# Squares behind the first turned tiles, held token loads, and other numbers for the planner, in a two-layer attention and feed-forward kernel

## The chip, the cores and the metric

The kernel runs on one core of one Trainium2 chip. A core has five engines with a queue of instructions each: PE (TensorE, matrix products), DVE (VectorE), ACT (ScalarE), POOL (GpSimd) and SP (SyncE, which here only starts DMAs). Each works its own queue strictly in order; semaphores make one engine wait for another or for a DMA. The metric is the time of one execution on the device, in microseconds (us), as the median of several runs.

## The reference, cut to what matters

Two equal layers over x, 2048 tokens by 576. Each layer adds a sliding, dilated attention and then a feed-forward network with SiLU:

```python
x = x + _A_ref(_layernorm(x), A_wqkv, A_wo)
x = x + _B_ref(_layernorm(x), B_w1, B_w2)
x = x + _A_ref(_layernorm(x), A_wqkv, A_wo)
x = x + _B_ref(_layernorm(x), B_w1, B_w2)

# _A_ref: 32 heads of 18; each token looks at 8 tokens, itself and every second one before it
logits = einsum("bhsd,bhswd->bhsw", q, kg) * scale     # then softmax over w
o = einsum("bhsw,bhswd->bhsd", attn, vg)               # then o @ wo
# _B_ref: silu(x @ w1) @ w2, with 4608 hidden features
```

All data are float32.

## The kernel before, in words

**Tiles and stages.** The 2048 tokens are four chunks of 512 (blocks of even and odd tokens), each of four tiles of 128. A stage `s` counts chunks over both layers, 0 to 7: `front(s)` does layer norm, attention and projection, `ffn(s)` the feed-forward network. Products need float32's accuracy from float16 operands, so every operand is split in a high half (ACT, `hi`) and a low half, the residue (DVE, `lo` or `halves_lo` at L344); each product is then three passes, 14 matrix instructions for a 128-token tile ("a product" below).

**Weights of attention.** `wqkv` is cut into four units of eight heads. `raw_wq(u)` loads a unit in five pieces (the last in two halves), squares each on ACT (L474), sums the squares on PE (L480), takes a power-of-two scale `su` on DVE (L484 to 486), and splits the pieces (hi L491 on ACT, lo L494 on DVE). Buffers: units 0 and 1 lie raw in `h` tiles and split in `wq` tiles; unit 2 is split into the `wo` tile, unit 3 into `h` tiles.

**Layer norm.** `layer_norm` takes statistics on DVE (L384, L385), an inverse root by Newton steps on DVE, then per tile y (ACT L431 or DVE L423), yh's halves (ACT L434 and DVE L344, or all DVE), and turns the tile: `transposed` either does nine 128x128 turns on PE (L357) with a copy by ACT (L359), or one turning DMA on SP (L361). `PE_LN` says which, for chunks 0 to 3 of layer 1. y and yh have two buffers each.

**Stage 0 computes ahead.** Beside chunk 0's own attention, the queries, keys and values of chunks 1 to 3 are computed with each unit's weights (`qkv_ahead`, products L566, evictions L579) and stored to DRAM. For chunk 0 each unit's keys (`kv`) get a halo by four DMAs that ACT starts (L645), and DVE does the logits (multiply L664, sum L668, twice), softmax and the weighted values (L697, L704, L705). Then come projection (`project`, L736), layer norm, and FFN 0, which loads and splits w1 and w2 while it runs (`raw_load`, `raw_split`) and stores the halves; later FFNs load them (L748, L753). A product with w1 is a "z" (L861, 14 instructions), one with w2 a group of 18 (L882, "mm2").

**What sets the order.** Nothing is written in its final order. `op(engine, duration, fn, reads, writes, prio, nbytes, after)` records an operation with an estimated duration; `Plan.order()` then plays a list schedule with these estimates: an engine takes the ready operation of lowest `prio` for which buffers are free. DMAs are played too: they start `DMA_IN` after their issue, share `DMA_RATE` between queues, and land `DMA_OUT` after their last byte. The order in which operations start in this play is the order in which they are emitted, and each engine then keeps its part of it. `after` only bars an operation from starting earlier in the play; on the chip only true dependencies are waited for. `gate` lists layer norm's low halves, `marks` small copies on POOL that do read data and so do hold POOL's queue.

Of the kernel before, what the change touches and what calls it, by code (L numbers as in the profile page):

```python
# [16 lines left out]
P = 128  # L17
# [8 lines left out]
NJ = 4  # L26
# [24 lines left out]
class Plan:  # L51
# [4 lines left out]
    DMA_IN, DMA_OUT = 1.2, 0.9  # L56
    DMA_RATE = 0.33e6
# [174 lines left out]
def sliding_attention_silu_ffn(ctx: ExitStack, tc: tile.TileContext, x, wqkv, wo, w1, w2, out):  # L232
# [8 lines left out]
    def fl(t):  # L241
        return t.rearrange("p a b -> p (a b)")
# [5 lines left out]
    def T(b):  # L248
        return S.tags[b.tag][b.slot]
# [98 lines left out]
    def transposed(src, dst, key, j, prio, on_pe=False):  # L348


        if on_pe:
            m = Buf("acc")

            def turn():
                t = fl(T(m).bitcast(F16))
                for k in range(9):
                    nc.tensor.transpose(t[:, k * P:(k + 1) * P], T(src)[:, k, :], ident)  # L357
            op("PE", 0.8, turn, [(src, 0), (src, 1)], [m], prio)
            return op("ACT", 1.05, lambda: nc.scalar.activation(  # L359
                dst(), fl(T(m).bitcast(F16))[:, 0:9 * P].rearrange("p (a b) -> p a b", a=9), AF.Copy), [m], [(key, j)], prio - 9)  # L360
        return op("SP", 1.7, lambda: nc.sync.dma_start_transpose(dst(), fl(T(src))), [(src, 0), (src, 1)], [(key, j)], prio,  # L361
                  nbytes=P * 9 * P * 4)


    PE_LN = (1, 1, 1, 0)
# [95 lines left out]
    def raw_wq(u):  # L461
# [4 lines left out]
        for k in range(5):  # L466
            def load(k=k):
                d = raw(k).rearrange("p (t c) -> p t c", t=3)
                for p0, n, row in ((0, P, k * P),) if k < 4 else ((0, 64, 512), (64, 64, 512)):
                    (nc.sync if u else nc.scalar).dma_start(d[p0:p0 + n], wqkv[row:row + n, :].rearrange(  # L470
                        "p (t c) -> p t c", t=3)[:, :, u * UC:(u + 1) * UC])

            def square(k=k):
                nc.scalar.activation(junk[:, :QR], raw(k), AF.Square, accum_out=accq[:, u, k:k + 1])  # L474
            op("SP" if u else "ACT", 0.8 if k < 4 else 1.3, load, [], [rs[k]], WQ[u] if u else -20, nbytes=P * 3 * UC * 4, after=gate[3:4] if u > 1 else ())
            op("ACT", 0.8, square, [rs[k]], [("accq", u, k)], WQ[u])
# [120 lines left out]
    def attention(s, xT, wq, more=None):  # L597
# [4 lines left out]
        for u in range(NU):  # L602
# [11 lines left out]
            else:  # L614
# [13 lines left out]
                for j in range(NJ):  # L628
                    m = Buf("misc")

                    def evac(j=j, m=m, u=u, kv=kv, qt=qt):
                        d = du[:, u:u + 1]
                        nc.scalar.activation(T(kv)[:, j + W - 1].rearrange("p a b -> p (a b)"), T(m)[:, UC:3 * UC],  # L633
                                             AF.Copy, scale=d)
                        nc.scalar.activation(T(qt)[:, j, :], T(m)[:, 0:UC], AF.Copy, scale=d)
                    op("PE", 2.7 if s else 2.9, lambda j=j, m=m, w=w: qkv_matmul(xT, w, j, m),
                       [(xT, j)] + w.keys, [m], pr_)
                    op("ACT", 0.9, evac, [m, ("su", u)], [(kv, j), (qt, j)], pr_ - (0 if s else 9))
# [73 lines left out]
    def project(s, o, xs):  # L712

        pr_ = s - 1.0
        for j in range(NJ):
# [22 lines left out]
            op("PE", 3.5, mm, [(oT, j)] + [(WO, k) for k in range(10)], [acc], pr_)  # L738
# [94 lines left out]
    def ffn(s, xT, xs):  # L833
# [4 lines left out]
        for g in range(NFT // n):  # L838
# [8 lines left out]
            for f in range(g * n, (g + 1) * n):  # L847
# [14 lines left out]
                op("PE", 3.05, mm, [(xT, j) for j in range(NJ)] + ka, [z], pp)  # L862
# [8 lines left out]
            for j in range(NJ):  # L871
# [4 lines left out]
                for hs_ in ((0,), (1,)) if last else ((0, 1),):  # L876
                    for t in range(0, n, step):
# [7 lines left out]
                        op("PE", 0.37 * step * len(hs_), mm2, [(hb[q], a) for q in range(t, t + step) for a in range(2)]  # L885
# [48 lines left out]
    def front(s):  # L934
        X[s] = load_x(s, s - 1.0 if s else -20)
        if s == 0:
            no_keys()
            xT = layer_norm(X[0], -20, "xa", 3, PE_LN[0])
            x1 = layer_norm(load_x(1, -8.5, gate[0:1]), -8.5, "xb", False, PE_LN[1])
# [6 lines left out]
            o = attention(0, xT, raw_wq, more)  # L946
# [48 lines left out]
```

## Time and profile before

| | |
|---|---|
| median of 3 runs | 2225.29 us (2223.28 to 2235.29) |
| the profiled execution | 2231.58 us, of which 2229.8 us span |
| PE busy | 2180.4 us, 98% |
| DVE busy | 1393.3 us, 62% |
| ACT busy | 747.4 us, 34% |
| POOL busy | 206.3 us, 9% |

The durations come from the profiled execution. Busy shares are means over stages: the page's slices show DVE at 8 or 9 tenths over the first fifth of the span and lower later. In a timeline a row gives start, length, engine, line, operation, output and input tiles, and in brackets how long the engine idled before it and what ended that.

### The profile page before, as it was taken

Reading aid. Unit: us, or ns where it says so; the run is one execution under the profiler, and the core shown is the slowest. Engines: PE = TensorE matmul, PEld = TensorE weight load, DVE = VectorE, ACT = ScalarE, POOL = GpSimd, SP = SyncE. Lnnn points to the kernel's source line nnn. Section 1 sums busy time; section 2 is a strip of 40 time slices with the busy share of each in tenths; the row PEclk is TensorE's granted clock in tenths of the full one; section 3 lists DMA queues with packets and bytes.
Section 4 is the critical chain, followed back from the end, with each engine's and each line's share of the span. In section 5 each row is a group of like instructions: output and inputs, shape, how many; then the busy total and the mean of one; then the engine's idle time right before and its main releaser. Section 6 shows DMA issues by size and latency. Waiting matters only on the chain.

```text
span 2229.8 us, 33919 instructions
## 1 busy us (share of the span) xinstructions
PE 2180.4 (98%) x13858; PEld 1350.7 (61%) x13858; DVE 1393.3 (62%) x2047; ACT 747.4 (34%) x1211; POOL 206.3 (9%) x341
## 2 busy tenths in 40 slices
PE   5999999999999999999999999999999999999999
PEld 3556565656666666655666656666666566666665
DVE  7999989889988311359834597336971389511111
ACT  6455777543132122224212232222322223222222
POOL 2133555200001000000000000000000000000000
PEclk9999999999999999999999999999999999999999
DMA  5577667784645433455445454454453643433331
GB/s 152 165 206 274 235 224 240 200 231 155 184 152 154 116 103 105 150 128 178 116 112 160 103 176 121 125 159 131 135 132 120 167 140 117 91 115 123 112 113 40
DMA packets 220564, 332.18 MB, mean 149 GB/s; under 512 B 107240, under 2 KB 127572, under 8 KB 216440
## 3 DMA queue, kind: packets, MB, share of 16 engines
q1 hardware_dynamic: 191408, 230.47, 36.4%
q0 software_dynamic: 20704, 78.02, 10.3%
q10 hardware_dynamic: 8296, 21.52, 3.5%
q8 instruction: 108, 1.77, 0.3%
q14 instruction: 48, 0.39, 0.1%
HBM read 240.08 MB, written 47.03 MB: 129 GB/s over the span
## 4 chain that ended last, share of the span: by engine, by line
PE 85%; DVE 6%; DMA 4%; issue 2%; ACT 1%; POOL 1%; ACTq 0%; SPq 0%; DVEq 0%; POOLq 0%
PE z L861 36%; PE acc L882 34%; PE misc L566 7%; PE acc L736 4%; PE z L566 3%; DMA w<-in_B_w_dram 1%; DVE pr L664 1%; DMA kv<-kv 1%; DVE pr L697 1%; DVE lg L668 1%; DMA oT<-yh 1%; DMA h<-in_A_wqkv_dram 1%; DVE x L743 0%; DVE w L807 0%; DVE pr L704 0%
## 5 line engine op out<-in xcount | busy, mean ns | idle before, releaser
L861 PE MATMUL z<-xb,w 128*128 128x512 f16 x4032 | 882.8, 380 | 7.9 <-issue 3.9
L882 PE MATMUL acc<-w,h 128*128 128x288 f16 x6912 | 856.1, 286 | 2.2 <-DVE h L868 1.3
L882 PEld LDWEIGHTS <-h 128*128 128x128 f16 x6912 | 676.4, 98 | 179.9 <-DVE h L868 1.6
L861 PEld LDWEIGHTS <-w 128*128 128x128 f16 x4032 | 394.8, 98 | 475.7 <-issue 6.7
L863 ACT ACTIVATE hs<-z,d 128x512 f32<-128x512 f32 x288 | 197.6, 686 | 979.9 <-PE z L861 962.2
L868 DVE SCALAR_TENSOR_TENSOR h<-hs,sh,h 128x512 f16<-128x512 f32 x288 | 213.8, 748 | 311.7 <-ACT h L865 311.6
L743 DVE SCALAR_TENSOR_TENSOR x<-acc,d,x 128x576 f32<-128x576 f32 x135 | 109.9, 814 | 325.1 <-PE acc L882 325.0
L664 DVE TENSOR_TENSOR pr<-qt,kv 128x2304 f32<-128x2304 f32 x64 | 163.3, 2551 | 89.3 <-DMA kv<-kv 66.4
L865 ACT ACTIVATE h<-hs,sh 128x512 f16<-128x512 f32 x288 | 207.5, 721 | 9.4 <-DVE d L830 0.3
L566 PEld LDWEIGHTS <-xa 128*128 128x128 f16 x1344 | 131.7, 98 | 121.2 <-issue 7.1
L566 PE MATMUL misc<-wq,xa 128*128 128x432 f16 x1008 | 190.0, 349 | 3.8 <-ACT xa L359 2.5
L697 DVE TENSOR_TENSOR pr<-kv,pe 128x1152 f32<-128x1152 f32 x128 | 169.0, 1352 | 1.2
L668 DVE TENSOR_REDUCE lg<-pr 128x128 f32<-128x2304 f32 x64 | 163.1, 2548 | 1.2
L704 DVE TENSOR_TENSOR pr<-pr 128x1152 f32<-128x1152 f32 (+1 forms) x128 | 135.1, 1056 | 3.5
L736 PE MATMUL acc<-wo,oT 128*128 128x288 f16 x896 | 114.8, 288 | 4.6 <-DMA oT<-yh 4.6
L736 PEld LDWEIGHTS <-oT 128*128 128x128 f16 x896 | 88.3, 99 | 30.1 <-DMA oT<-yh 4.9
L633 ACT ACTIVATE kv<-misc,du 128x288 f32<-128x288 f32 x80 | 40.0, 500 | 138.5 <-PE misc L566 79.6
L906 POOL DMA_DIRECT2D out_dram<-x x12 | 6.5, 546 | 698.3 <-DVE x L743 698.3
L687 ACT ACTIVATE pe<-lg 128x256 f32<-128x256 f32 x32 | 13.3, 416 | 169.2 <-DVE lg L678 161.3
L566 PEld LDWEIGHTS <-xb 128*128 128x128 f16 x448 | 43.7, 98 | 38.6 <-ACT xb L359 0.9
L384 DVE BATCH_NORM_STATS2 st<-x 128x6 f32<-128x288 f32 x128 | 52.0, 448 | 10.9 <-DMA x<-in_A_x_dram 5.9
L743 DVE SCALAR_TENSOR_TENSOR x<-acc,so,x 128x576 f32<-128x576 f32 x32 | 26.1, 815 | 29.5 <-PE acc L736 29.4
(121 smaller groups left out, 1127.4 us busy)
## 6 DMA issues: line engine op xcount, KB each, us to landing
w<-w1s SPq DMA_DIRECT2D x252, 320.0 KB
w<-w2s SPq DMA_DIRECT2D x252, 288.0 KB
wq<-wqs SPq DMA_DIRECT2D x17, 1080.0 KB
kv<-kd POOLq DMA_DIRECT2D x8, 1584.0 KB, 8.2
w1s<-w POOLq DMA_DIRECT2D x36, 320.0 KB, 4.2
w<-in_B_w_dram POOLq DMA_DIRECT2D x36, 288.0 KB, 5.3
w2s<-w POOLq DMA_DIRECT2D x36, 288.0 KB, 4.2
kv<-kv ACTq DMA_DIRECT2D x20, 504.0 KB
```

Source lines behind the costliest of these rows:

```text
L566: nc.tensor.matmul(T(m)[:, :3 * UC], a, b, start=n == 0, stop=n == len(pl) - 1)
L664: nc.vector.tensor_tensor(T(pr), T(qt)[:, j:j + 2, None, :].to_broadcast([P, 2, W, UC]), win(T(kv), j, 2), op=ALU.mult)
L668: nc.vector.tensor_reduce(T(lg)[:, j:j + 2].rearrange("p a w h -> p (a w h)"), T(pr).rearrange("p a w (h d) -> p (a w h) d", d=DH), axis=A ...
L697: nc.vector.tensor_tensor(T(pr)[:, a].rearrange("p w (h d) -> p w h d", d=DH), v, T(pe)[:, j + a, :, :, None].to_broadcast([P, W, UH, DH]) ...
L704: nc.vector.tensor_tensor(t[:, :, 0:h, :], t[:, :, 0:h, :], t[:, :, h:2 * h, :], op=ALU.add)
L736: nc.tensor.matmul(T(acc)[:, h, 0:288], a, b[:, h * 288:(h + 1) * 288], start=n == 0, stop=n == len(pl) - 1)
L743: nc.vector.scalar_tensor_tensor(t, T(acc)[:, :, 0:288], d, t, op0=ALU.mult, op1=ALU.add)
L861: nc.tensor.matmul(T(z), v, u, start=m == 0, stop=m == len(pl) - 1)
L863: op("ACT", 0.7, lambda z=z, hs=hs, f=f: nc.scalar.activation(T(hs), T(z), AF.Silu, scale=d1[:, f:f + 1]), [z, ("s12", f)], [hs], pd, tabl ...
L865: op("ACT", 0.72, lambda hs=hs, h=h, f=f: nc.scalar.activation(T(h)[:, 0, :], T(hs), AF.Copy, scale=shs[i][:, f:f + 1]), [hs, ("sh", i, g) ...
L868: op("DVE", 0.75, lambda hs=hs, h=h, f=f: nc.vector.scalar_tensor_tensor(T(h)[:, 1, :], T(hs), shs[i][:, f:f + 1], T(h)[:, 0, :], op0=ALU. ...
L882: nc.tensor.matmul(T(acc)[:, h, 0:288], T(hb[q])[:, a, j * P:(j + 1) * P], T(wbs[q][0])[:, w, h * 288:(h + 1) * 288], start=q == 0 and m = ...
```

## The change

It has four parts.

1. The squares of units 1 to 3 may start in the plan only behind the copies of chunk 0's four turned tiles (`turned`, a list that `transposed` fills).
2. Unit 0's loads go from ACT's queue to SP's, behind chunk 0's tokens. Chunk 1's tokens stay on POOL's queue, and a new copy `g0` on POOL ahead of them reads unit 0's scale, so that POOL does not start them before it exists. For this unit 0's `raw_wq` is recorded before chunk 1's load.
3. Chunk 2's tiles are turned by DMA instead of on PE (`PE_LN`).
4. The planner's numbers: transfers land 1.8 instead of 0.9 us after their last byte at 0.29 instead of 0.33 MB per us, and five durations on PE are a little smaller.

```diff
-    DMA_IN, DMA_OUT = 1.2, 0.9
-    DMA_RATE = 0.33e6
+    DMA_IN, DMA_OUT = 1.2, 1.8
+    DMA_RATE = 0.29e6
...
-            return op("ACT", 1.05, lambda: nc.scalar.activation(
+            o = op("ACT", 1.05, lambda: nc.scalar.activation(
                 dst(), fl(T(m).bitcast(F16))[:, 0:9 * P].rearrange("p (a b) -> p a b", a=9), AF.Copy), [m], [(key, j)], prio - 9)
+            turned.append(o)
+            return o
...
-    PE_LN = (1, 1, 1, 0)
+    turned = []
+    PE_LN = (1, 1, 0, 0)
...
-                    (nc.sync if u else nc.scalar).dma_start(d[p0:p0 + n], wqkv[row:row + n, :].rearrange(
+                    nc.sync.dma_start(d[p0:p0 + n], wqkv[row:row + n, :].rearrange(
...
-            op("SP" if u else "ACT", 0.8 if k < 4 else 1.3, load, [], [rs[k]], WQ[u] if u else -20, nbytes=P * 3 * UC * 4, after=gate[3:4] if u > 1 else ())
-            op("ACT", 0.8, square, [rs[k]], [("accq", u, k)], WQ[u])
+            op("SP", 0.7 if k < 4 else 1.3, load, [], [rs[k]], WQ[u], nbytes=P * 3 * UC * 4, after=gate[3:4] if u > 1 else ())
+            op("ACT", 0.8, square, [rs[k]], [("accq", u, k)], WQ[u], after=turned[:NJ] if u else ())
...
-                op("PE", 3.05, mm, [(xT, j) for j in range(NJ)] + ka, [z], pp)
+                op("PE", 3.03, mm, [(xT, j) for j in range(NJ)] + ka, [z], pp)
...
-            x1 = layer_norm(load_x(1, -8.5, gate[0:1]), -8.5, "xb", False, PE_LN[1])
+            w0 = raw_wq(0)
+            g0 = op("POOL", 0.2, lambda: nc.gpsimd.tensor_copy(pace, su[0:1, 0:1]), [("su", 0)], ["pace"], -18)
+            x1 = layer_norm(load_x(1, -8.5, [g0]), -8.5, "xb", False, PE_LN[1])
...
-            o = attention(0, xT, raw_wq, more)
+            o = attention(0, xT, lambda u: raw_wq(u) if u else w0, more)
```

Lines below 944 of the new kernel are numbered three higher than before from L364 on.

**ACT, just behind unit 0's squares.** `h_114` to `h_118` are unit 0's pieces, `h_119` to `h_122` four of unit 1's, `x_66` chunk 0's first tile. Before:

```order
L474 ACTIVATE junk,accq<-h_118 128x432
L474 ACTIVATE junk,accq<-h_119 128x432
L474 ACTIVATE junk,accq<-h_120 128x432
L474 ACTIVATE junk,accq<-h_121 128x432
L474 ACTIVATE junk,accq<-h_122 128x432
L431 ACTIVATE y_90<-x_66,nt_131 128x576
L434 ACTIVATE yh_92<-y_90,nt_131 128x576
L491 ACTIVATE wq_77<-h_114,su 128x432
```

After:

```order
L477 ACTIVATE junk,accq<-h_118 128x432
L434 ACTIVATE y_90<-x_66,nt_131 128x576
L437 ACTIVATE yh_92<-y_90,nt_131 128x576
L494 ACTIVATE wq_77<-h_114,su 128x432
L494 ACTIVATE wq_77<-h_115,su 128x432
L494 ACTIVATE wq_77<-h_116,su 128x432
L494 ACTIVATE wq_77<-h_117,su 128x432
L359 ACTIVATE xa_74<-acc_135 128x9x128
```

Four squares of unit 1 that stood between unit 0's squares and tile 0's y have gone down the queue, behind the four copies into `xa`.

**ACT, around unit 0's halo.** `kv_79` holds unit 0's keys and values of chunk 0 and `kv_80` unit 1's, `x_71` to `x_73` are chunk 2's later tiles, and `h_114` to `h_118` by now take unit 3's halves. Before:

```order
L635 ACTIVATE qt_82<-misc_137,du 128x144
L645 DMA kv_79<-kv_79 112x1152
L645 DMA kv_79<-kv_79 15x1152
L645 DMA kv_79<-kv_79 112x864
L645 DMA kv_79<-kv_79 14x864
L633 ACTIVATE kv_80<-misc_138,du 128x288
L635 ACTIVATE qt_82<-misc_138,du 128x144
L491 ACTIVATE h_114<-w_108,su 128x432
```

After:

```order
L494 ACTIVATE h_118<-w_112,su 128x432
L434 ACTIVATE y_91<-x_71,nt_131 128x576
L437 ACTIVATE yh_93<-y_91,nt_131 128x576
L434 ACTIVATE y_90<-x_72,nt_131 128x576
L648 DMA kv_79<-kv_79 112x1152
L648 DMA kv_79<-kv_79 15x1152
L648 DMA kv_79<-kv_79 112x864
L648 DMA kv_79<-kv_79 14x864
L437 ACTIVATE yh_92<-y_90,nt_131 128x576
L434 ACTIVATE y_91<-x_73,nt_131 128x576
L648 DMA kv_80<-kv_80 112x1152
```

The halo of unit 0 stood ahead of unit 3's splitting; it now stands behind it and behind y of chunk 2's third tile, and the second halo ahead of yh of the fourth.

**DVE, at attention's first multiply** (`pr<-qt,kv`). Before:

```order
L494 SCALAR_TENSOR_TENSOR h_118<-w_112,su,h_118 128x432
L664 TENSOR_TENSOR pr_87<-qt_81,kv_79 128x2304
L344 SCALAR_TENSOR_TENSOR yh_93<-y_91,nt_131,yh_93 128x512
L344 SCALAR_TENSOR_TENSOR yh_93<-y_91,nt_131,yh_93 128x64
L344 SCALAR_TENSOR_TENSOR yh_92<-y_90,nt_131,yh_92 128x512
L344 SCALAR_TENSOR_TENSOR yh_92<-y_90,nt_131,yh_92 128x64
L668 TENSOR_REDUCE lg_84<-pr_87 128x128
```

After:

```order
L497 SCALAR_TENSOR_TENSOR h_118<-w_112,su,h_118 128x432
L344 SCALAR_TENSOR_TENSOR yh_93<-y_91,nt_131,yh_93 128x512
L344 SCALAR_TENSOR_TENSOR yh_93<-y_91,nt_131,yh_93 128x64
L344 SCALAR_TENSOR_TENSOR yh_92<-y_90,nt_131,yh_92 128x512
L344 SCALAR_TENSOR_TENSOR yh_92<-y_90,nt_131,yh_92 128x64
L344 SCALAR_TENSOR_TENSOR yh_93<-y_91,nt_131,yh_93 128x512
L344 SCALAR_TENSOR_TENSOR yh_93<-y_91,nt_131,yh_93 128x64
L667 TENSOR_TENSOR pr_87<-qt_81,kv_79 128x2304
L671 TENSOR_REDUCE lg_84<-pr_87 128x128
```

All residues of chunk 2 now stand ahead of the first multiply, where two pairs stood behind it and two further down.

**SP, at chunk 1's second layer norm** (`xb_76`, the operand of FFN 1; `w1s` and `w2s` are its weights). Before:

```order
L748 DMA w_97<-w1s_160 128x1280
L361 DMA_TRANSPOSE xb_76<-yh_93 128x9x128
L748 DMA w_99<-w1s_161 128x1280
L361 DMA_TRANSPOSE xb_76<-yh_92 128x9x128
L748 DMA w_100<-w1s_162 128x1280
L361 DMA_TRANSPOSE xb_76<-yh_93 128x9x128
L361 DMA_TRANSPOSE xb_76<-yh_92 128x9x128
L753 DMA w_103<-w2s_198 128x1152
```

After:

```order
L363 DMA_TRANSPOSE xb_76<-yh_92 128x9x128
L363 DMA_TRANSPOSE xb_76<-yh_93 128x9x128
L363 DMA_TRANSPOSE xb_76<-yh_92 128x9x128
L363 DMA_TRANSPOSE xb_76<-yh_93 128x9x128
L751 DMA w_99<-w1s_157 128x1280
L756 DMA w_108<-w2s_193 128x1152
```

The four turns stand together ahead of the first load of FFN 1's weights, where eleven loads stood ahead of the last turn. On PE, chunk 1's projection moves up as well: it stood behind 30 z and 36 mm2 groups of FFN 0, and stands behind 26 and 32.

## Rows read from the trace of the kernel before

**Rows 1.** The page, busy us (share of the span) and instructions.

```profile
PE 2180.4 (98%) x13858; PEld 1350.7 (61%) x13858; DVE 1393.3 (62%) x2047; ACT 747.4 (34%) x1211; POOL 206.3 (9%) x341
```

**Rows 2.** PE's waits: engine, line, waited for, us in total, times, longest.

```profile
PE acc L736 <- DMA oT<-yh: 4.6, 1, 4.6
```

**Rows 3.** Stretches: length, each engine's busy us, PEclk, DMA share, GB/s.

```profile
200.00:300.00 100.00, 96.02 (x634) 59.69 (x633) 94.66 (x160) 67.50 (x117) 43.78 (x77) 1.00 0.71 240
500.00:800.00 300.00, 300.00 (x1959) 191.50 (x1957) 226.78 (x295) 83.44 (x112) 10.16 (x16) 1.00 0.50 151
```

**Rows 4.** The chain that ended last, first 60 us: start, us, what.

```profile
10.85 6.75 DMA h<-in_A_wqkv_dram
...
19.73 0.67 ACT y L431
...
21.21 2.18 ACT wq L491 x4
...
48.08 2.56 PE z L566 x14
```

**Rows 5.** Timeline of the first 45 us, all engines.

```profile
10.12 3.99 SPq L470 DMA_DIRECT2D h<-in_A_wqkv_dram  x6
...
14.63 0.15 DVE L330 TENSOR_SCALAR su<-p 128x1 int32<-128x1 int32 x1
...
22.10 2.40 DVE L494 SCALAR_TENSOR_TENSOR wq<-h,su,wq 128x432 f16<-128x432 f32 x4
...
25.47 5.22 PE L566 MATMUL misc<-wq,xa 128*128 128x432 f16 x14 [2.51 <-ACT xa L359]
```

**Rows 6.** Timelines of PE, ACT and DVE from 56 to 78 us.

```profile
58.13 0.28 PE L480 MATMUL misc<-accq,ones 128*128 128x5 f32 x2
...
56.45 2.84 ACTq L645 DMA_DIRECT2D kv<-kv  x3
60.00 1.20 ACT L491 ACTIVATE h<-w,su 128x432 f16<-128x432 f32 x2
66.53 4.15 ACTq L645 DMA_DIRECT2D kv<-kv  x4
...
64.03 2.55 DVE L664 TENSOR_TENSOR pr<-qt,kv 128x2304 f32<-128x2304 f32 x1
75.86 1.79 DVE L344 SCALAR_TENSOR_TENSOR yh<-y,nt,yh 128x512 f16<-128x512 f32 x4
```

**Rows 7.** Timelines of SP and ACT at chunk 3's turned tiles.

```profile
139.73 2.28 SPq L361 DMA_TRANSPOSE xa<-yh  x1
...
144.22 0.76 ACT L434 ACTIVATE yh<-y,nt 128x576 f16<-128x576 f32 x1
```

**Rows 8.** The chain that ended last, 300 to 480 us.

```profile
316.32 2.21 PE acc L882 x18
318.52 3.02 PE z L861 x14
...
327.82 0.81 DVE w L812
...
397.78 15.38 DMA oT<-yh
```

**Rows 9.** Two stretches behind long idle times of PE, columns as in rows 3.

```profile
413.20:416.60 3.40, 3.39 (x15) 2.15 (x16) 1.89 (x5) 2.31 (x5) 3.23 (x6) 0.50 1.17 301
474.80:478.20 3.40, 3.40 (x10) 1.20 (x9) 1.62 (x1) 0.00 (x0) 0.00 (x0) 0.53 1.03 409
```

**Rows 10.** Timelines of DVE, SP and PE in FFN 0.

```profile
321.70 0.16 DVE L329 TENSOR_SCALAR p<-misc 128x4 int32<-128x4 int32 x1 [2.71 <-PE misc L796]
395.07 1.80 DVE L344 SCALAR_TENSOR_TENSOR yh<-o,so,yh 128x512 f16<-128x512 f32 x4
...
456.49 6.07 SPq L361 DMA_TRANSPOSE xb<-yh  x2
...
474.45 5.73 PE L861 MATMUL z<-xb,w 128*128 128x512 f16 x18 [3.93 <-issue]
```

More of the change, by code (lines that the diff above doesn't have):

```diff
@@ L635, in evac @@
                         nc.scalar.activation(T(qt)[:, j, :], T(m)[:, 0:UC], AF.Copy, scale=d)
-                    op("PE", 2.7 if s else 2.9, lambda j=j, m=m, w=w: qkv_matmul(xT, w, j, m),
+                    op("PE", 2.6, lambda j=j, m=m, w=w: qkv_matmul(xT, w, j, m),
                        [(xT, j)] + w.keys, [m], pr_)
@@ L737, in mm @@
                                          start=n == 0, stop=n == len(pl) - 1)
-            op("PE", 3.5, mm, [(oT, j)] + [(WO, k) for k in range(10)], [acc], pr_)
+            op("PE", 3.47, mm, [(oT, j)] + [(WO, k) for k in range(10)], [acc], pr_)
             op("DVE", 0.85, lambda j=j, acc=acc: add_to(xs[j], acc, DO), [acc, "so"], [xs[j]], pr_ - 0.3)
@@ L884, in mm2 @@
                                                          start=q == 0 and m == 0, stop=q == n - 1 and m == 2)
-                        op("PE", 0.37 * step * len(hs_), mm2, [(hb[q], a) for q in range(t, t + step) for a in range(2)]
+                        op("PE", 0.365 * step * len(hs_), mm2, [(hb[q], a) for q in range(t, t + step) for a in range(2)]
                            + [k for q in range(t, t + step) for k in wbs[q][1]], [(acc, h) for h in hs_], pp)
```

## The prediction

> **What bounds the kernel now.** I began with the page's busy shares: PE works 2180.4 us of a span of 2229.8 [rows 1], so an edit that only moves work can win or lose PE idle time, of which there are some 49 us. In the view of PE's waits the one large piece behind the start that has a name is 4.6 us for a turned tile of a projection [rows 2]. The stretches tell the stages apart [rows 3]. From 200 to 300 us PE (96.0) and DVE (94.7) are both full; from 500 to 800 us PE is busy for every microsecond and DVE for three quarters. So only the first 475 us or so can change the end, and in their long middle **two engines bound it together**: PE can use a lead only if DVE has it too.
>
> The chain of waits names the head's path [rows 4]: the load of a piece of unit 1's weights (6.75 us from 10.85, landed at 17.6), ACT's squares of it, then at 19.73 y, at 21.21 the splitting of unit 0's weights. PE's first real products start at 25.47 and take 5.22 us for 14 [rows 5], where the same 14 later take 2.56 [rows 4].
>
> **Part 1, the squares.** Unit 1's squares leave ACT's path. y of tile 0 then needs only chunk 0's statistics and unit 0's squares, and what is late next is unit 0's scale, su.
>
> **Part 2, queues and hold.** Before, unit 0's loads (ACT's queue) ran beside chunk 0's tokens, SP could issue unit 1's loads only from 10.12 on, and su was there at 14.8 [rows 5]. Now SP issues chunk 0's four tiles, then unit 0's six pieces at 3.99/6 = 0.67 us each [rows 5], and chunk 1's tokens wait on Pool for su; nothing else is queued behind them on Pool that is wanted before. I take su at 12.1, 2.7 us sooner. No row shows these loads alone; the bounds are 0 and 4 us, the time of six issues. From 12.1 on ACT does y and yh of tile 0 (1.5, from 19.73 to 21.21 in [rows 4]) and four splits (2.2). DVE follows with the residue of tile 0 (0.9), those of the four splits (2.4, [rows 5]) and tile 1's halves (1.3), which end near 18.2; tile 1's turn stands before the first product on PE. So that starts near 18.5 instead of 25.47: **7 us gained**.
>
> In the new order PE then has chunk 0's four products, chunk 1's turns and four products, and unit 1's four products of chunk 0, with nothing else between: 5.2 + 11 x 2.56 and some 5 us of turns, sums and one wait for a copy make 38.4 us, and unit 3's sum of squares comes at 56.9. Before, it ended at 58.4 [rows 6] with nine products done. PE's lead is 1.5 + 3 x 2.56 = **9.2 us**.
>
> **Part 3, where the lead goes.** Chunk 2's tiles are now turned by DMA on SP, and the rows of ACT and DVE around them change. Unit 3's scale is ready at 57.9, a microsecond behind its sum. From there ACT does five splits at 0.6, 2.9 [rows 6]; y and yh of tile 1, 1.5; y of tile 2, 0.7; the halo's four issues, 3.5 (three of them took 2.84, and ACT's next instruction starts only when they are out, [rows 6]); yh of tile 2, 0.8; y of tile 3, 0.7; the second halo, 4.15 [rows 6]; an eviction and yh of tile 3, 1.4. That is 73.6. DVE has tile 3's residue done 0.9 later, and only behind that, at 74.5, stands attention's first multiply, which started at 64.03 [rows 6]. The four residues of chunk 2 (3.6 us) are then done, which used to lie among the logits: before, residues and both pairs of logits were done at 77.65 [rows 6]; now at 74.5 + 4 x 2.55 = 84.7. **DVE is 7.0 us late.** Bounds: 3.5, if the first halo's issue costs DVE nothing, and 11.2, if another of 4.15 falls in.
>
> PE loses its lead at the same place. Chunk 2's four products of unit 0 stand one behind the other, each waiting for its turned tile. One DMA turn was there at most 4.5 us after its start (139.73 to 144.22, when ACT writes its source buffer again, [rows 7]), another 15.38 us after [rows 8]; I take 4.5, the nearer row, since here the halos are all that runs beside it. The tiles land at 63.3, 67.7, 72.8 and 79.0, PE would be free at 62.2, 65.9, 70.3 and 75.4: 1.1 + 1.8 + 2.5 + 3.6 = 9.0 us of idling. The 36 turns that PE no longer does are worth nothing while DVE is the later one.
>
> **Part 4, up to FFN 0.** Attention of chunk 0 follows on DVE in nearly the same order as before and keeps it full until the projection, so the 7.0 us arrive there: **+7.0**. PE, with nothing of its own left, idles before that projection. An idle of over 4 us was followed by 3.4 us at a granted 0.50, the 1.2 GHz level [rows 9]: **+1.7**. In FFN 0 DVE at places waits for PE, longest 2.71 at 321.70 [rows 10]; a late DVE finds the answer there: **-2.7** (bounds 0 and twice that).
>
> **Part 5, the planner's numbers.** Later landings and trimmed durations do no work; they move rows. Two moves matter. SP now turns chunk 1's four normalized tiles ahead of all of FFN 1's loads. Before, the last turn was issued in the 6.07 us from 456.49, and PE's first product on these tiles began at 474.45 after 3.93 us of idling for which the profile has no name [rows 10]; by elimination it waited for that turn. This idle and the 1.7 of slow clock behind it [rows 9] go: **-5.6**. And chunk 1's projection stands four z and four mm2 groups earlier on PE, 4 x 3.02 + 4 x 2.21 = 20.9 us [rows 8], while DVE has ahead of its residues there (at 395.07, [rows 10]) only 15 pieces of about 0.81 less [rows 8] and one multiply more, 9.6 us. So PE may arrive up to 11.3 us too soon; the low end is 0, if the plan has both right. Nearest is the wait that this projection had, 4.6 [rows 2]; I take it once more: **+4.6**.
>
> The page Advanced Engine Details and Errata of the Trainium skill (X-Bar Transpose (TRN2)) says that turning transfers are as fast as plain ones. By its 350 GB/s a tile of 295 kB would need an estimated 0.8 us; then the wait at 474.45 would not be the turn's and the sum would come out 5.6 us higher. The 15.38 us of [rows 8] speak against it where other transfers run.
>
> **The sum:** 7.0 + 1.7 - 2.7 - 5.6 + 4.6 = +5.0 us. The profiled execution took 2231.58, so 2236.6 of its kind; the median of the runs, 2225.29, lies 6.3 lower, which gives **2230.3 us**.
>
> **The rivals.**
> - *The lead stays.* If DVE is not held behind chunk 2's residues (its first multiply starts before 67.6, which is 64.03 plus the 3.6 moved ahead of it), PE keeps 9.2 and the 5.6 comes on top: 2225.3 - 14.8 = 2210.5. For it: DVE's waits for PE in FFN 0 [rows 10] mean that it is not the limit everywhere. Against: two halos stand ahead of the last yh on an in-order ACT.
> - *Projection 1 stands too early (slower than before).* If PE waits there the whole 11.3 instead of 4.6, with one more slow stretch of 1.7, the sum is +13.4: 2238.7. It decides from the point where DVE's residues there end less than a turn, 4.5 us, before PE arrives. For it: 9.6 against 20.9. Against: the plan knows both engines' work.
> - *The hold brings nothing.* If unit 0's loads land no sooner behind the tokens on one queue, su stays at 14.8, only the squares are won, and all behind is 2.7 later than I have it: 2233.0.
>
> **How the numbers follow.** Forecast 0.50, lead stays 0.22, projection too early 0.20, idle hold 0.08. The forecast's own bounds: low 3.5 + 1.7 - 5.4 - 5.6 + 0 = -5.8 (2219.5), high 11.2 + 1.7 - 0 - 5.6 + 11.3 = +18.6 (2243.9). Reaching down to 2213 it takes in the nearer half of the first rival, and 2213 to 2243 leaves out about 2 in 10. Half a per cent, 11.1 us, is about what a measurement of this kernel can tell from no change. Beyond it on the fast side lies some half of the first rival: 0.12. On the slow side lies most of the second and the forecast's upper end: 0.19. Within it: 0.69.
>
> **What would show it.** Right: the first 14 products near 18.5 and su near 12.1 (parts 1, 2); DVE's first multiply of attention near 74.5 and four waits of PE between 62 and 81 (part 3); an idle of PE ahead of projection 0 with 0.50 behind it (part 4); no idle before FFN 1's first product, a wait at projection 1's first tile (part 5). Wrong at once: a first multiply before 68, or PE without idle between 62 and 81.

## The result, and the profile of the changed kernel

| | before | changed |
|---|---|---|
| median of 13 runs each | 2225.82 us | 2236.97 us |
| lowest to highest | 2219.84 to 2235.29 | 2235.08 to 2243.53 |
| the profiled execution | 2231.58 | 2235.08, of which 2233.3 span |

The ratio is 1.0048, interval 1.0035 to 1.0060: 11 us slower, inside the range of 2213 to 2243 and within the half per cent, 6.7 us above the 2230.3 forecast. Two things in the table matter for what follows. Before's runs are spread over 15 us, those of the changed kernel, but for one, over 3.4. And the two profiled executions are only 3.5 us apart. Of 17 runs of before that stand beside the first experiments, the nine below 2226 us have a mean granted clock (of TensorE, as a share of full speed) of 0.999 or 1.000, the eight above 2227 one of 0.998.

The page of the changed kernel, as in [rows 1]: PE does the same work, less 36 turns.

```profile
PE 2179.7 (98%) x13822; PEld 1349.3 (60%) x13822; DVE 1394.5 (62%) x2047; ACT 748.6 (34%) x1211; POOL 205.1 (9%) x342
```

PE's waits of the changed kernel (columns as in [rows 2]). Only the first wait of the kernel, 11.9 us for unit 0's squares, is longer than these. Waits for turned tiles head the list again, but the tiles are chunk 2's, and no wait of projection 1 is left.

```profile
PE z L569 <- DMA xb<-yh: 11.5, 3, 8.5
PE z L864 <- DVE w L810: 6.0, 3, 2.9
PE misc L799 <- ACT junk L794: 5.9, 2, 5.4
PE z L864 <- ACT hs L866: 4.5, 3, 2.6
```

Timelines of the changed kernel, all engines, in order of time: the scale su (14.63 before, [rows 5]), PE's first product (25.47, [rows 5]), unit 3's sum of squares (58.13, [rows 6]); the second and third of chunk 2's four turns on SP (the first was issued at 57.29, the fourth at 76.50), the second halo's last three DMAs on ACT (the first of its four took another 2.31 from 64.02) and, in a narrower window, the last of them alone, PE's long wait, what ACT did behind the halo, the last residue and the first multiply of attention (64.03, [rows 6]), PE's next wait; PE's idle time ahead of projection 0, DVE's residues of that projection, and FFN 0's first z.

```profile
12.96 0.15 DVE L330 TENSOR_SCALAR su<-p 128x1 int32<-128x1 int32 x1
18.82 4.30 PE L569 MATMUL misc<-wq,xa 128*128 128x432 f16 x14
55.27 0.28 PE L483 MATMUL misc<-accq,ones 128*128 128x5 f32 x2
61.52 8.10 SPq L363 DMA_TRANSPOSE xb<-yh  x2
66.37 7.76 ACTq L648 DMA_DIRECT2D kv<-kv  x3
73.32 0.81 ACTq L648 DMA_DIRECT2D kv<-kv  x1
73.35 4.33 PE L569 MATMUL z<-wq,xb 128*128 128x432 f16 x14 [8.50 <-DMA xb<-yh]
74.18 0.62 ACT L582 ACTIVATE w<-z,du 128x432 f32<-128x432 f32 x1 [8.82 <-DMA xb<-yh]
75.49 0.95 DVE L344 SCALAR_TENSOR_TENSOR yh<-y,nt,yh 128x512 f16<-128x512 f32 x2 [9.82 <-ACT yh L437]
76.36 2.55 DVE L667 TENSOR_TENSOR pr<-qt,kv 128x2304 f32<-128x2304 f32 x1
79.64 10.62 PE L569 MATMUL z<-wq,xb 128*128 128x432 f16 x48 [1.96 <-DMA xb<-yh]
...
185.07 0.59 PE L799 MATMUL misc<-accw,ones 128*128 128x4 f32 x2 [5.40 <-ACT junk L794]
188.07 1.80 DVE L344 SCALAR_TENSOR_TENSOR yh<-o,so,yh 128x512 f16<-128x512 f32 x4
...
233.74 6.42 PE L864 MATMUL z<-xb,w 128*128 128x512 f16 x29
...
388.30 1.80 DVE L344 SCALAR_TENSOR_TENSOR yh<-o,so,yh 128x512 f16<-128x512 f32 x4
...
401.03 3.59 PE L739 MATMUL acc<-wo,oT 128*128 128x288 f16 x28
```

The last two are projection 1: DVE's residues and PE's first tile, with no idle time before it.

PE takes chunk 2's tiles in order, so its waits of 1.04 us (at 62.11), 8.50 and 1.96 are for the first, second and third turn. By the completion events in the trace the four turns landed 4.8, 11.8, 13.9 and 4.6 us after the start of their issue. The two slow ones each start 1.7 us behind the first DMA of a halo (59.79 and 64.02). The chain of waits has the third as one piece (start, us, what):

```profile
65.73 13.86 DMA xb<-yh
```

The halo's row of 7.76 us is not all issuing. Its three DMAs take 0.83, 1.81 and 0.81 us, and for 4.27, from 69.05 to 73.32, ACT issues nothing. The second turn landed at 73.30, and the halo's last DMA (73.32) and PE's product (73.35) both start then. In the trace they wait for the same completion semaphore: ACT's and SP's DMAs share eight of these, and the halo's last DMA had to take the one that the second turn still held. So a DMA can wait for an earlier one with which it shares no data, and an engine here waits for more than true dependencies.

In the kernel before, projection 0's residues and FFN 0's first z, from its timelines:

```profile
181.82 1.80 DVE L344 SCALAR_TENSOR_TENSOR yh<-o,so,yh 128x512 f16<-128x512 f32 x4
...
224.12 12.25 PE L861 MATMUL z<-xb,w 128*128 128x512 f16 x56
```

Up to FFN 0's first z both kernels have done the same products (but for the 36 turns), so 233.74 against 224.12 is the balance up to there: the 6.7 us by which PE's first product came sooner are gone and 9.6 more are lost. The rest is in the stretches (columns as in [rows 3]), first the changed kernel, then before. PE idles 12.9 instead of 7.1 us in 240 to 400, which is FFN 0, and in 400 to 480, where before lost 8.7 us, not at all.

```profile
185.60:189.00 3.40, 3.40 (x11) 1.40 (x10) 3.33 (x6) 0.00 (x0) 3.40 (x7) 0.50 0.90 244
240.00:400.00 160.00, 147.09 (x930) 91.14 (x930) 152.50 (x224) 109.45 (x197) 82.40 (x144) 0.99 0.71 237
400.00:480.00 80.00, 80.00 (x537) 52.29 (x536) 72.83 (x134) 50.39 (x84) 24.94 (x44) 1.00 0.80 220
```

```profile
240.00:400.00 160.00, 152.93 (x974) 94.66 (x973) 148.67 (x234) 114.91 (x205) 88.03 (x154) 1.00 0.70 231
400.00:480.00 80.00, 71.27 (x477) 47.31 (x475) 65.87 (x110) 33.53 (x54) 15.45 (x28) 0.96 0.85 212
```

### The profile page after: what moved, and what is told of

The parts are those of the page before. It is cut to its first block, busy times and chain, and to the rows that moved or that the text cites. A ratio compares the mean times of both kernels' runs of the same rounds, so it can differ in the third digit from the quotient of the medians.

```text
span 2233.3 us, 33834 instructions
## 1 busy us (share of the span) xinstructions
PE 2179.7 (98%) x13822; PEld 1349.3 (60%) x13822; DVE 1394.5 (62%) x2047; ACT 748.6 (34%) x1211; POOL 205.1 (9%) x342
## 4 chain that ended last, share of the span: by engine, by line
PE 89%; DVE 5%; DMA 3%; issue 1%; ACT 1%; POOL 0%; ACTq 0%; SPq 0%; DVEq 0%; POOLq 0%
PE z L864 37%; PE acc L885 37%; PE misc L569 9%; PE acc L739 4%; PE z L569 2%; DVE pr L700 1%; DMA w<-in_B_w_dram 1%; DVE pr L667 1%; DVE pr L707 1%; DMA xb<-yh 1%; DVE lg L671 1%; DMA h<-in_A_wqkv_dram 0%; DMA wqs<-h 0%; DVE w L810 0%; DMA w2s<-w 0%
## 5 line engine op out<-in xcount | busy, mean ns | idle before, releaser
L569 PE MATMUL z<-wq,xb 128*128 128x432 f16 x224 | 45.0, 364 | 12.2 <-DMA xb<-yh 11.5
```

Of the source, the lines that this page charges most:

```text
L569: nc.tensor.matmul(T(m)[:, :3 * UC], a, b, start=n == 0, stop=n == len(pl) - 1)
```

## The experiments

Two questions were open: why the medians lie 11 us apart and the profiles 3.5, and which part costs it. Ratios are against runs of the kernel before on the same chip. Line numbers of the variants differ by a few.

### The kernel before, a second profile

No edit.

> The kernel before, once more, unchanged. Its runs lie between 2219.8 and 2235.3 us, those of the changed kernel but for one between 2235.1 and 2238.5. Theory (two flickering waits): the profiled execution shown, 2231.6, paid PE's 4.63 us for a turned tile of projection 1, the 3.93 us before FFN 1's first product and 1.7 us of slow clock behind each, 12.0 in all; an execution near 2220 pays neither, one near 2226 about half. The head and the rest of PE's idle times agree within 1 us. Rival (spread everywhere): this execution differs from the one shown by many small pieces, and the two waits stand in both, 4.6 and 3.9.

It ran in 2225.16 us, 6.4 less than the execution shown, and has the same 13858 matrix instructions in the same order, so the two can be laid over each other row by row. The second one is 1.25 us ahead from the first instructions of PE on, 2.75 more at FFN 1's first product, 1.7 more in the four microseconds behind it, and little anywhere else. PE's timeline, its wait for turned tiles, and the stretch behind FFN 1's first product:

```profile
24.19 5.22 PE L566 MATMUL misc<-wq,xa 128*128 128x432 f16 x14 [2.51 <-ACT xa L359]
...
470.45 1.89 PE L861 MATMUL z<-xb,w 128*128 128x512 f16 x8 [1.14 <-issue]
```

```profile
PE acc L736 <- DMA oT<-yh: 4.7, 2, 2.4
```

```profile
470.40:473.80 3.40, 3.35 (x16) 1.59 (x17) 3.37 (x2) 0.12 (x1) 0.54 (x1) 1.00 1.02 392
```

The theory was half right. Projection 1's wait stands in both (4.6 and 4.7). FFN 1's, 3.93 with half clock behind it [rows 9, 10], is 1.14 here and the granted clock stays at 1.00. By the completion events PE waits there for the last turn of `xb`, which took 14.4 us from issue to landing in the first profile and 11.6 in the second. **This execution, which lies at the median, did not have most of that loss.**

### Part 3 undone

```diff
-    PE_LN = (1, 1, 0, 0)
+    PE_LN = (1, 1, 1, 0)
```

> The changed kernel with chunk 2's tiles turned on PE again (part 3 undone). Theory (turning transfers and halos hold each other up): the three waits of PE for turned tiles, 11.5 us between 62 and 80, are gone; three DMAs of the second halo issue in about 3 instead of 7.76 us; DVE's first multiply of attention starts near 70 instead of 76.4, oT's residues 6 us earlier than the 188.1 after; 2229 to 2231 us. Rival (the order of rows is to blame, not the transfers): all residues of chunk 2 stand ahead of the first multiply here too, so it starts at 75 or later and the time stays within 2 us of 2237.

2229.46 us, ratio 1.0027 (1.0012 to 1.0042): by the medians part 3 costs 7.5 of the 11 us; by the ratios, which take in this kernel's three runs above 2234 us, 4.7. From the timelines, the second halo (the first and the last of its four DMAs; 0.83 and 0.80 the two between), the first multiply, the residues of projection 0 and FFN 0's first z, which comes 6.05 us sooner than in the changed kernel:

```profile
66.82 1.23 ACTq L648 DMA_DIRECT2D kv<-kv  x1
...
69.92 0.81 ACTq L648 DMA_DIRECT2D kv<-kv  x1
72.35 2.56 DVE L667 TENSOR_TENSOR pr<-qt,kv 128x2304 f32<-128x2304 f32 x1 [1.34 <-DMA kv<-kv]
...
185.81 1.80 DVE L344 SCALAR_TENSOR_TENSOR yh<-o,so,yh 128x512 f16<-128x512 f32 x4
...
227.69 6.42 PE L864 MATMUL z<-xb,w 128*128 128x512 f16 x29
```

The same four DMAs take 3.67 us instead of 10.07 (5.8 without the wait for the turn), and PE waits 3.4 us for turned tiles in 62 to 80 instead of 11.5. That settles the theory for PE. For DVE both sides were partly right: the first multiply comes 4 us sooner, but still 8.3 behind before's. Its row says that it waits for a halo, the first, which ACT issues from 62.92 on (55.79 before); that order of rows comes with the new head, not with part 3. oT's residues gain only 2.3; no run here shows why.

### Part 4 undone, and part 4 alone

```diff
-    DMA_IN, DMA_OUT = 1.2, 1.8
-    DMA_RATE = 0.29e6
+    DMA_IN, DMA_OUT = 1.2, 0.9
+    DMA_RATE = 0.33e6
```

(and the five durations).

> The changed kernel with the planner's old numbers (part 4 undone). Theory (the numbers help in the changed kernel): up to 190 us as the changed kernel; then the waits at projection 1 and before FFN 1's first product come back, 4 to 12 us with their slow clock: 2241 to 2249 us. Rival (the numbers bring the waits of PE for DVE's split weights in FFN 0, 12.8 us after against 7.0 before between 240 and 385): these fall back to 7 or less, and the time to 2228 to 2231.

2238.87 us, ratio 1.0060 (1.0039 to 1.0080), not to be told from the changed kernel, so neither theory. The turned-tile wait of projection 1 is back, as 2.1 and 1.4, the one of FFN 1 is not:

```profile
PE acc L739 <- DMA oT<-yh: 3.5, 2, 2.1
```

> The kernel before with the planner's new numbers alone (part 4 alone). Theory (the numbers take the two flickering waits away and cost nothing): no idle time of PE over 2 us between 400 and 480, runs near 2220 and within 4 us of each other. Rival (they move FFN 0's weights so that PE waits for DVE): waits of PE between 240 and 385 grow from 7.0 to 12 or more, which leaves 2226 to 2231. Third case: they do nothing with this head, 2225.8.

2249.03 us, ratio 1.0106 (1.0086 to 1.0126). No theory had this: the numbers alone make the kernel before 23 us slower. The rival had the place, FFN 0, but not the size. FFN 0's stretch and PE's waits:

```profile
240.00:400.00 160.00, 141.05 (x898) 87.59 (x896) 149.43 (x230) 104.80 (x185) 77.56 (x136) 0.98 0.66 214
```

```profile
PE acc L882 <- DVE h L868: 6.3, 5, 2.5
PE z L861 <- ACT hs L863: 5.6, 4, 2.5
```

PE idles 19 of 160 us there, and the longest groups of waits are short ones for DVE and ACT, none for a DMA. So what seven numbers do to the time depends on the order that they meet: 23 us in the kernel before, nothing that can be told with the other three parts.

### Parts 1 and 2 alone

The diff's squares, queues and hold on the kernel before, nothing else.

> Parts 1 and 2 alone on the kernel before (squares, queues, hold), chunk 2 on PE and the planner's numbers as before. Theory (parts 3 and 4 act apart): part 3 cost 7.5 us with the new numbers, so its undoing here saves as much from the 2238.9 of the old numbers: 2231 us, and the waits of projection 1, 2 to 4 us, are there as in the kernel before. Rival (the head brings its 6.6 us once nothing later spoils it): 2219 us. Third case (the head's gain is lost to DVE alone): DVE's first multiply of attention at 70 or later, as with the new numbers (72.4), and oT's first residues of chunk 0 no earlier than the 181.8 before.

2232.41 us, ratio 1.0026 (1.0014 to 1.0038), as the first theory had it, and by the third case: DVE is late although chunk 2's tiles are not turned by DMA here.

```profile
70.45 2.56 DVE L667 TENSOR_TENSOR pr<-qt,kv 128x2304 f32<-128x2304 f32 x1 [1.12 <-DMA kv<-kv]
...
183.27 1.80 DVE L344 SCALAR_TENSOR_TENSOR yh<-o,so,yh 128x512 f16<-128x512 f32 x4
```

Su is there at 12.5 and PE's first product starts at 18.2, 7.2 and 6.0 us ahead of the two profiles of before; oT's residues are 1.5 and 3.1 us behind them. A faster head alone is 6 us slower.

### Without the hold

```diff
-            g0 = op("POOL", 0.2, lambda: nc.gpsimd.tensor_copy(pace, su[0:1, 0:1]), [("su", 0)], ["pace"], -18)
-            x1 = layer_norm(load_x(1, -8.5, [g0]), -8.5, "xb", False, PE_LN[1])
+            x1 = layer_norm(load_x(1, -8.5, gate[0:1]), -8.5, "xb", False, PE_LN[1])
```

> The changed kernel without the hold: the small copy on POOL that reads unit 0's scale is left out, so chunk 1's tokens start some 5.5 us sooner, beside unit 0's loads. Theory of the change (the hold keeps the queues free for unit 0): su comes later than 13.0, by 1 us or more, and PE's first product later than 18.8. Rival (the hold brings nothing, the order on SP alone does): su and first product within 0.3 us, time within 2 us of 2237.

2239.06 us, ratio 1.0052 (1.0040 to 1.0065). Su's row starts at 12.30, PE's product at 18.16, both some 0.7 us sooner than with the hold; that is inside the 1.25 by which the head differs between two profiles of before. The hold brings nothing; the order on SP and the moved squares, which were not run apart, do it.

```profile
12.30 0.15 DVE L330 TENSOR_SCALAR su<-p 128x1 int32<-128x1 int32 x1
```

### The halo first, by its priority

```diff
-                op("ACT", 3.2, halo, own, [(kv, "halo")], pr_ - 0.2, nbytes=P * 14 * UC * 4)
+                op("ACT", 3.2, halo, own, [(kv, "halo")], pr_ - (9 if s == 0 and u == 0 else 0.2), nbytes=P * 14 * UC * 4)
```

> The changed kernel with the halo of chunk 0's first unit sent as soon as its keys are there (a lower priority number for that one operation). Theory (DVE is late since the halo and all residues of chunk 2 stand ahead of the first multiply): the first multiply starts before 60 instead of at 76.4, oT's first residues come 6 us or more before 188.1, PE's idle time of 5.4 us ahead of projection 0 goes; PE's wait for turned tiles (11.5) stays or shrinks by the halo's share; 2225 to 2230 us. Rival (PE's waits for the turned tiles set the time, DVE's lateness is hidden): 2235 to 2237.

> The same halo edit with chunk 2's tiles turned on PE (part 3 undone as well; that alone gave 2229.5). Theory: both losses gone, the head's lead of some 6 us kept by PE and DVE: 2216 to 2222 us, first multiply before 60. Rival (DVE is full from 60 to 190 whatever its start, and FFN 0 waits for DVE later): 2226 to 2230.

2258.39 us (ratio 1.0150, 1.0130 to 1.0170), and 2249.03 (1.0099, 1.0084 to 1.0114) with chunk 2 on PE: neither theory. The first one's timelines:

```profile
47.73 2.55 DVE L667 TENSOR_TENSOR pr<-qt,kv 128x2304 f32<-128x2304 f32 x1
...
174.60 1.80 DVE L344 SCALAR_TENSOR_TENSOR yh<-o,so,yh 128x512 f16<-128x512 f32 x4
...
235.92 0.68 ACT L796 ACTIVATE junk<-w 128x576 f16<-128x576 f32 x1 [5.90 <-DMA w<-in_B_w_dram]
240.24 2.32 PE L569 MATMUL z<-wq,xa 128*128 128x432 f16 x6 [10.25 <-ACT hs L582]
```

DVE did come 28.6 us earlier to its first multiply and 13.5 to oT's residues. But the planner made another order of everything behind it: PE idles 10.25 us for an eviction that stands on ACT behind a square whose weights have not landed. Such an edit does not test one wait. So the next kernels keep the finished order and move single rows in it.

### The halo first, rows moved by hand

```diff
-    for o in S.order():
+    seq = S.order()
+    for o, b in pin + [(first[0], gate[9]), (first[1], gate[10]), (first[2], first[1]), (first[3], first[2])]:
+        seq.remove(o)
+        seq.insert(seq.index(b) + 1, o)
+    for o in seq:
         o.fn()
```

`pin` holds the first halo and its unit's last eviction, `first` the first two multiplies and sums; the first kernel moves the halo alone.

> The changed kernel in its own order, row by row, but for the four halo DMAs of chunk 0's first unit: they stand on ACT behind that unit's last eviction (near 33 us) instead of behind y of chunk 2's third tile. Nothing else moves on any engine, unlike in the kernel with the new priority, where the planner moved hundreds of rows. Theory (halos and turning transfers hold each other up): the third tile's turn lands some 4 us sooner and PE's 8.5 us wait there falls to 3 to 5; the second halo's three DMAs issue in under 5 instead of 7.76 us; DVE's first multiply starts near 71; 2231 to 2234 us. Rival (the second halo alone sets the last residue): first multiply still past 74.5, 2236 to 2238.

> The same, and on DVE the first multiply and sum of attention moved up behind the residues of chunk 2's second and third tiles, into time in which DVE idled (3.3 us from 61.4 and 9.8 from 65.7 in the changed kernel). Theory (DVE's lateness at its first multiply is what reaches projection 0): first multiply near 61.5, oT's first residues of chunk 0 at 178 to 180 instead of 188.1, PE's idle of 5.4 us with 1.8 of slow clock before projection 0 gone; 2224 to 2230 us. Rival (as in the kernel with the new priority, whose first multiply came at 47.7 and whose time was 2258: a DVE that is early only waits in FFN 0): PE's waits between 240 and 385 stay at 12 or grow, 2233 or more.

> The same two moves in the order of the kernel that has chunk 2 turned on PE (2229.5). Theory: its 8.4 us of idling of PE in 160 to 182, for evictions and a turned tile that wait for DVE and ACT, go with DVE's lateness; first multiply near 62; 2218 to 2224 us, faster than the kernel before. Rival (those waits have other causes: stores, the DMA turn of chunk 3): 2226 to 2230.

2239.05 us (1.0050, 1.0038 to 1.0062), 2239.88 (1.0056, 1.0040 to 1.0071) and 2238.75 (1.0060, 1.0042 to 1.0079; the unpinned one had 2229.46). The first came out by its rival, with the first multiply at 74.99; the theories of the other two failed, and the rival of the second has the time but not the reason, since no early DVE reached FFN 0. The second kernel's timelines show why:

```profile
37.41 3.06 PE L570 MATMUL z<-wq,xb 128*128 128x432 f16 x8 [4.10 <-ACT xb L359]
...
67.93 2.56 DVE L670 TENSOR_TENSOR pr<-qt,kv 128x2304 f32<-128x2304 f32 x1
96.55 0.62 DVE L690 TENSOR_REDUCE mx<-pe 128x32 f32<-128x256 f32 x1 [8.85 <-ACT pe L695]
190.64 1.80 DVE L344 SCALAR_TENSOR_TENSOR yh<-o,so,yh 128x512 f16<-128x512 f32 x4
```

The halo's issue stands at 33 us in front of copies that PE waits for (4.10, half clock behind it: PE is 6.6 us later by unit 3's sum). And the multiply, 8.4 us earlier, leads to an exponential that ACT still has in its old place behind evictions: DVE waits 8.85 and has nothing left. In the first kernel no halo starts ahead of the second turn any more, and it landed 4.5 us after its issue instead of 11.8. The second halo's last three issues, no longer parted by a wait, took 4.5 us instead of 7.76, as its theory said of them. PE's long wait moved from chunk 2's second tile to its third (9.19 at 83.37), whose turn starts 1.7 us behind the second halo as before and took 13.95 us. This bears out that halos and turns hold each other up.

What else can be read: with PE's order the same, oT's residues come 2.0, 2.6 and 9.2 us later than in the unpinned kernels, FFN 0's first z 2.3, 3.3 and 9.2 later, and the medians 2.1, 2.9 and 9.3. The medians are the weaker evidence, since the runs of before beside these three had 2227.66, some 1.8 us more than those beside the unpinned ones; against them it is 0.2, 1.1 and 7.5. In the traces it is not PE's delay that goes through to FFN 0 (5.3 and 6.6 by unit 3's sum in the first two) but nearly DVE's at oT's residues. These are delays; that a lead goes through too, they don't show.

### Halos on SP, exponentials moved along

```diff
-                        nc.scalar.dma_start(t[p0 + d:p0 + d + n, i:i + m], t[p0:p0 + n, 11 - m:11])
+                        (nc.scalar if s else nc.sync).dma_start(t[p0 + d:p0 + d + n, i:i + m], t[p0:p0 + n, 11 - m:11])
```

> The order of the kernel with chunk 2 turned on PE (2229.5), pinned row by row, with the rows moved that held DVE back there: the four units' halos of stage 0 are sent by SP, each behind its unit's last eviction, and no longer stand on ACT; DVE's first two multiplies, their sums and the first softmax stand right behind chunk 2's residues; the four exponentials of stage 0, and y and yh of chunk 3's tiles, stand one to five rows earlier on ACT, where DVE then asks for them. PE's order is untouched. Theory (DVE's lateness at the softmax of unit 0, 91.5 us there, reaches projection 0 one to one, as 2.0 and 2.6 us did with the moved halo): first multiply near 64.5, softmax's sum of unit 0 near 83, oT's first residues at 178 to 180 instead of 185.8, PE's idle times of 4.1 and 3.0 between 162 and 182 mostly gone: 2221 to 2225 us. Rival (the time is set behind 190 us, by FFN 0's weights, and DVE's lead turns into waits there): oT's residues at 180 or before, and still 2228 to 2231 us.

In this kernel the exponentials of units 1 to 3 stand ahead of the second sum of their logits, so these weights are others than the reference's, and that sum on DVE waits for the exponential (4.77 and 1.48 us) instead of the other way round. 2234.19 us, ratio 1.0031 (1.0019 to 1.0043). Its timelines:

```profile
108.07 2.55 DVE L677 TENSOR_REDUCE lg<-pr 128x128 f32<-128x2304 f32 x1 [4.77 <-ACT pe L698]
...
183.50 1.80 DVE L344 SCALAR_TENSOR_TENSOR yh<-o,so,yh 128x512 f16<-128x512 f32 x4
...
398.45 6.25 PE L751 MATMUL acc<-wo,oT 128*128 128x288 f16 x28 [5.51 <-DMA oT<-yh]
```

The first multiply comes at 64.4 and the softmax at 83.3, as expected; of the 8.1 us the misplaced exponentials take 6.3, and oT's residues keep 2.3. PE's order is that of the kernel it was made from, so the two can be laid over each other. PE leads by some 2.3 us through FFN 0 and by 4.0 at its end, until projection 1, where it now waits 5.51 and 1.10 for turned tiles and runs at half clock behind that: the lead became a lag of 5.6. The turns did not start late: on SP's timeline they start 4 us sooner than in the unpinned kernel (381.83 against 385.85). Nor did PE come sooner behind DVE's residues: 12.1 us, against 11.9 there. But the first two turns took 16.6 and 21.1 us from issue to landing instead of 7.3 and 6.4. The chain of waits from 370 to 412 us (start, us, what) leads through the second:

```profile
384.69 21.07 DMA oT<-yh
```

Plain transfers beside them were slow as well: three loads of FFN weights from POOL's queue, 288 KB each and so as large as a turn, took 12.2 to 14.3 us, in the unpinned kernel 5.6 to 6.1. The rows are this kernel's (from 382.9 to 384.7 us), then that of the unpinned one (385.2 to 388), with the median us from issue to landing:

```profile
w<-in_B_w_dram POOLq DMA_DIRECT2D x3, 288.0 KB, 12.7
```

```profile
w<-in_B_w_dram POOLq DMA_DIRECT2D x3, 288.0 KB, 6.1
```

So the theory holds up to projection 1. The end is neither its rival nor the prediction's second one, in which PE stands there too early; it is the time that these transfers took, which the order of rows does not fix.

## Why the prediction was right, and which steps were not

**Head (parts 1, 2): right.** First product 18.82 (18.5 said), unit 3's sum at 55.27 (the sum done at 55.6; 56.9 said), so PE's lead was 10.5 us instead of 9.2. Su came at 13.0, not 12.1, and not through the hold, which brought nothing: the third rival's name for it was true, its condition (su stays at 14.8) was not.

**Where the lead goes (part 3): right in place, with two prices wrong.** First multiply 76.36 (74.5), DVE late at projection 0 by 6.25 (7.0), PE idle for chunk 2's turned tiles 11.5 (9.0). But the 9.0 were four growing waits of 4.5 us turns; there were three, of 1.04, 8.50 and 1.96. The failed steps are two prices, "I take 4.5, the nearer row" for a turn and "the second halo, 4.15". The first and the fourth turn took 4.8 and 4.6 us, but the second and third, right behind the start of a halo, 11.8 and 13.9; and the second halo took 10.07, of which 4.27 are ACT's wait for the second turn. Each price came from a row in which the other was absent. That the first multiply still came within 2 us of the forecast is in part luck: the prediction's own sum has the second halo start at 68.0, and it started at 64.02. PE's half clock behind the two longer waits (0.50 in 73.4 to 76.6, 0.51 in 80.0 to 83.4) stands in no term; whether it cost anything while DVE was the later engine, no run tells.

**Up to FFN 0 (part 4): right, then wrong.** The idle time ahead of projection 0 (5.40 and 0.72) and its 1.8 of half clock are there, and FFN 0's first z comes 9.6 late (7.0 + 1.7 said). The step "a late DVE finds the answer there", -2.7, failed: idling in FFN 0 grew by 5.8, where PE now waits for DVE's split weights (6.0, before 2.2) and for ACT (4.5, before 1.6), and another 3.3 us run at half clock (0.50 in 291.8 to 295.1).

**Part 5: one right, one wrong.** No idle before FFN 1's first product, -5.6 as said. Projection 1, +4.6, failed: PE reached it at 401.0, 12.7 us behind DVE's residues there (388.30) instead of 9.9 as before (395.07, [rows 10], against 404.99), and did not wait; with the half clock behind it that is -6.3. PE's later coming is only part of it. The first two turns landed 5.1 and 4.7 us after their issue, before 8.1 and 15.4 [rows 8]; a second turn of 15.4 would have landed at 407.1, where PE began the second tile at 404.6. The two wrong terms nearly cancel, by luck: +1.9 said, -0.5 measured.

So the sum, +5.0, stands against 3.5 between the two profiled executions. The measured pieces (9.6, 5.8, -5.6, -6.3) give 3.5 too, but they leave out FFN 0's half clock, 1.7, so they are good to about 2 us. **What made the forecast 6.7 us low is the last line of the sum**: "the median of the runs, 2225.29, lies 6.3 lower". I took this offset as a constant of both kernels. It was the price of waits that one execution of before paid and another did not: 4.5 of 6.4 are FFN 1's first wait and its half clock, the very loss that the sum also took away as won, at 5.6. The same loss was subtracted twice. This rests on one second profile, at the median, and on the clocks of the 17 runs. Without it the working gives 2230.3 + 4.5 = 2234.8, and the changed kernel's median lies 1.9 above its own profile, not 6.3 below.

The Trainium skill (Advanced Engine Details and Errata, X-Bar Transpose (TRN2)) has turning transfers as fast as plain ones. No run times the two alone. Beside each other at projection 1, turns took 7.3 and 6.4 us and plain loads of the same size 5.6 to 6.1 in the kernel without part 3, and 16.6 and 21.1 against 12.2 to 14.3 in the last variant. So here turns were somewhat slower, and both kinds slowed down together. The prediction's estimate by that section of the Trainium skill, 0.8 us for a tile, is not borne out either: the fastest turn looked at here took 3.2 us, and PE's wait at 474.45 was for a turn of 14.4. The measurements decide.

The Trainium skill's Perfetto Trace Analysis (DMA Instruction — HWDGE (DVE, Sync)) says that an issue in the profile includes waiting for the lock of a descriptor generator, which DVE's and Sync's sequencers share. The second halo's four issues add up to 5.8 us on ACT beside SP's turns, and to 3.67 without them, which would agree with sharing between ACT and SP; no run here separates it from full queues.

**Open.** Whether DVE's 8 us, kept to projection 0, would make the new head pay: that was not run in a form that keeps the exponentials right. And why two turns at projection 1, with the same rows on SP, take 7 us in one kernel and 17 to 21 in another: the loads beside them were slow in the same stretch, but which of them holds up which is not shown. No kernel here was faster than the one before; the nearest are the new head alone, at 1.0026, and the one without part 3, at 1.0027.

## What to carry to other kernels

Before a profiled execution's offset from the median is carried over to a changed kernel, find what it consists of: profile the old kernel twice and lay the two over each other row by row. A wait that flickers must not be counted both as the offset and as a gain. And where a planner writes the order, an edit of its numbers or of one priority tests the whole new order (some 20 us here); to test one wait, pin the order and move the rows, with all that stands in line behind them on the in-order engines. Last, a row of a timeline that merges several DMAs can hold a wait between two of them; look at a narrower window before its length is taken for the time of issuing.

## What the runs showed of the hardware

- Four halo DMAs issue from ACT in 3.67 us, and in 5.8 while SP issues turning transfers; from SP, in the last variant, in 3.45 and 3.59.
- ACT's and SP's DMAs share eight completion semaphores in these traces, and a DMA waits for the earlier one on its semaphore: the second halo's last DMA stood 4.27 us for a turn that landed at 73.30.
- A turning transfer of one tile (295 kB) took 11.8 and 13.9 us from issue to landing when it started 1.7 us behind a halo, 4.8 and 4.6 otherwise, and 4.5 instead of 11.8 when the halo ahead of it was moved away. At projection 1 two turns took 7.3 and 6.4 us in one kernel and 16.6 and 21.1 in another; plain loads of the same size beside them took 6.1 and 12.7 in the median.
- PE's granted clock was 0.50, the 1.2 GHz level, behind idle times of 5.40, 5.51 and 2.86 us, and 1.00 behind one of 1.14; as before, 3.4 us at the lower level cost 1.7.
